# Pair 0 in transposed token order, a new order of all engines, and tiled matmuls grouped

## The chip, the cores and the metric

The kernel runs on one core of one Trainium2 chip. The metric is the device time of one execution in microseconds (us), as the median of several runs. Matmuls run on TensorE (PE; PEld is its loading of weights), copies, exps and gelus on ScalarE (ACT), element-wise work and 32x32 transposes on VectorE (DVE), some more on GpSimd (POOL). All transfers are issued by one queue, that of SyncE (SP).

## The reference

Batch `B = 8`, heads `H = 8`, tokens `S = 576`, head width 64. In each head 32 packed queries attend to all keys, and then the tokens attend to the 32 packed values. A gelu FFN over all 4608 tokens follows (`DM = 512`, `DFF = 2048`).

```python
p_packed = sm_attn(p, k, v)                 # per head: [32, 64]
out = sm_attn(q, p_packed, p_packed)        # per head: [576, 64]
x = out.transpose(0, 2, 1, 3).reshape(B * S, H * D)
h = x @ w_in
g = 0.5 * h * (1 + erf(h / sqrt(2)))
return g @ w_out
```

## The kernel before

**Units and steps.** Work is cut into 4 pairs of batches and 4 blocks of 512 columns of DFF, so 16 units `u` with 8 steps each: step `n` from 0 to 127, 32 of them a pair. The second softmax is never multiplied with the packed values: these are folded into `w_in` (`packed_w_in`, matmuls `wps` L960, split for precision into two parts `wp` by ACT L971 and DVE L976), and the hidden product `h` (L1026) multiplies the softmax weights `a2T` with `wp`. Per step, `h` goes through gelu on ACT (`graw` L1049), a cast (`g` L1056) and a subtraction on DVE (L1058), and four output tiles `o` of each batch (three matmuls each, L1079 to L1081) and one edge tile `o_edge` that both batches of a pair share are multiplied with `w_out`. DVE adds them up in `acc` (L1140), and the rows are stored (L1144).

**Attention of a pair.** `load` brings k and q (L383 for pair 0, L393 for the rest), `load_values` brings v (L440 and L442). PE computes the first scores (`s1`, in `products` L485), ACT their exps (`softmax`, L572), PE turns them (`e1T`, L593 and L596), multiplies them with v (`pp`, L631) and turns the result (L645); then come the second scores (`s2`, L485 again), the exps (L726), and the transposes on DVE (L744, L752) that make `a2`. Pair 0 reads k and q by rows and turns them on PE, so its tokens come out in another order than they have in memory; the exps L572 of pair 0 and the transposes `in_order` of L744 and L752 put them back in order. In the other pairs DVE turns 32x32 blocks. Until pair 0's `a2` is split into two parts, its first hidden products run unsplit in full fp32 (L1017, "plain").

**Tiled and whole matmuls.** The matmuls `s1`, `s2`, `pp` and `wps` use a part of PE's array each (the trace shows forms 64\*32 and 128\*32); all others use the whole array (128\*128).

**What sets the order.** Before anything is emitted, a planner written in Python (`class Order`) plays the kernel through: each piece is an `Op(engine, cost, step, fn, takes)`, `cost` being a guess in us. An engine that is free takes, of its ops whose inputs are there, the one with the lowest `step` for which the buffers (`Ring`s, with as many buffers as memory has room for) are free. Constants give the latency between engines, the rate of the transfers and the cost of a change of ACT's table. The tables `FIRST` (pair 0), `LATER` (pairs 1 to 3) and `LEAD` (weights) hold the `step` of each piece. The order that comes out is then fixed: on the chip each engine runs its own list and waits on semaphores.

**Idle matmuls.** While the planner has nothing for PE before time 150 and until the output has begun, `keep_warm` emits a matmul of zeros (L999) into the next free PSUM buffer. A tile first named by such a matmul keeps the name "idle". PSUM has the rings `psum_o` (four buffers, output tiles) and `wide` (two buffers, two banks each: `h`, scores, `e1T`, `pp`, `wps`).

Of the kernel before, what the change touches and what calls it, by code (L numbers as in the profile page):

```python
# [47 lines left out]
IDLE, IDLE_END = 0.11, 150.0  # L48

# [3 lines left out]
    "p": (-36.9, -24.7),  # L53
    "k": (19.1, -16.7, 9.7, 17.4),
    "v": (38.2, 48.4, 60.2, 73.6),
    "q": (19.5, 34.4, 60.7, 32.0),
    "scores1": (12.9, -36.2),
    "softmax1": (15.7, 19.0, 8.2, 16.7),
    "packed": (-24.6, -1.0, 7.5, 28.7),
    "scores2": (26.1, 14.1),  # L60
    "softmax2": (11.1, 33.2, 30.2, 70.4),
    "weights2": (29.1, 67.4, 29.6, 48.1),
    "groups1": ((0, 1, 2, 3),),
# [68 lines left out]
class Op:  # L132
# [3 lines left out]
    def __init__(self, engine, cost, step, fn, takes=(), table=None, busy=True, port=False):  # L136
        self.engine, self.cost, self.step, self.fn = engine, cost, step, fn
        self.takes, self.table, self.busy = takes, table, busy

        self.port = (engine == POOL and cost > 0) or port  # L140


class Order:
# [4 lines left out]
    def __init__(self):  # L148
# [5 lines left out]
        self.port = 0.0  # L154
# [60 lines left out]

    def issue(self, engine):
        ready = self.ready[engine]
        for i, (_, _, op, go_on, begin) in enumerate(ready):
            if not op.takes or all(r.has_room(name, n if r is op.takes[0][0] else 0) for n, (r, name) in enumerate(op.takes)):
                del ready[i]  # L220
                break
        else:
# [8 lines left out]
        if engine == DMA:  # L231
            n, size = op.cost
            end = self.now
            for _ in range(n):
                end = max(end, self.under_way[-DMA_DEPTH])
                self.link = max(self.link, end + DMA_ISSUE + DMA_START) + size / n / DMA_RATE
                end += DMA_ISSUE
                self.under_way.append(max(self.link, end + DMA_START) + DMA_END)
            done = self.under_way[-1]
        else:  # L240
# [7 lines left out]
            if engine == PE:  # L248
                end = begin + self.clock(begin, op.cost, op.busy)
# [21 lines left out]
def packed_attention_gelu_ffn(ctx: ExitStack, tc: tile.TileContext, q, k, v, p, w_in, w_out, out):  # L271
# [37 lines left out]
    vraws = ring("vraw", 1, [P, 20 * D])  # L309
# [4 lines left out]
    e1ts = ring("e1T", 1, [P, 5, P])  # L314
# [65 lines left out]
    def load(bt, name, src, c, step):  # L380
# [14 lines left out]
        cost, fn = ((1, 590e3), rows) if bt.b < 2 else ((4, 1475e3), blocks)  # L395
# [38 lines left out]

    def load_values(s, step):
        heads = slice(4 * s.hh, 4 * s.hh + 4)

# [6 lines left out]
        s.v = yield Op(DMA, (2, 660e3), step, fn, [(s.v_ring, f"v_{s.n}")])  # L444
# [82 lines left out]
    def scores1_of_chunk(s, step):  # L527
# [4 lines left out]
            PE, 0.68, step,  # L532
# [3 lines left out]
            [(wide, f"s1_{s.n}")], busy=False)  # L536
# [23 lines left out]
    def softmax1(ss, step):  # L560
# [6 lines left out]
        def exps():  # L567
            for s in ss:
                src, dst = s.e1, s.e1
                if s.b < 2:  # L570
                    src, dst = s.t1[:, :, :HALF].rearrange("p e (t x) -> p e t x", t=NT), rows_in_order(s.e1)
                nc.scalar.activation(dst, src, AF.Exp, bias=mx[:, 1, s.i:s.i + 1], scale=SCALE, accum_out=s.z)  # L572

        yield Op(ACT, (1.6 if ss[0].b < 2 else 0.76) * n, step, exps, table="exp")
# [11 lines left out]
    def packed(s, step):  # L586
# [4 lines left out]
        def most(t):  # L591
            for i in range(4):
                nc.tensor.transpose(bank(t)[:, i * P:(i + 1) * P], s.e1[:, i:512:4], ident)  # L593

        def least(t):
            nc.tensor.transpose(t[:64, :P], s.e1[:, 512:S], ident)  # L596

        def both(t):
            most(t)
            least(t[:, 1])  # L600

        def copy_most(t):
            nc.scalar.copy(e1T[:, 0:4].rearrange("p t n -> p (t n)"), bank(t))

        def copy_least(t):
            nc.scalar.copy(e1T[:64, 4], t[:64, :P])

        def copy_both(t):
            copy_most(t)
            copy_least(t[:, 1])  # L610
# [605 lines left out]
```

## Time and profile before

| | |
|---|---|
| median of three runs | 743.86 us (742.77 to 744.17) |
| span of the profiled execution | 741.7 us |
| median of the runs less that span | 2.16 us |
| PE busy | 730.1 us, 98% |
| DVE, ACT, POOL busy | 396.2, 351.8, 155.7 us |
| transfers | 106.77 MB, mean 144 GB/s |

The span goes from the first to the last instruction of one profiled execution; the runs are whole executions. "Busy" counts from an instruction's start to its end, and the ends of matmuls are modelled, so a PE that is busy all the time can still lose time between matmuls. What a group of matmuls costs is therefore read from the starts: from its own to that of the next matmul. A row of a timeline holds start, length, engine, line, operation, output and inputs, the form of the matmul (rows\*columns of the array), the tile, and behind "x" how many records are in it.

### The profile page before, as it was taken

Reading aid. Unit: us, or ns where it says so; the run is one execution under the profiler, and the core shown is the slowest. Engines: PE = TensorE matmul, PEld = TensorE weight load, DVE = VectorE, ACT = ScalarE, POOL = GpSimd, SP = SyncE. Lnnn points to the kernel's source line nnn. Section 1 sums busy time; section 2 is a strip of 40 time slices with the busy share of each in tenths; the row PEclk is TensorE's granted clock in tenths of the full one; section 3 lists DMA queues with packets and bytes.
Section 4 is the critical chain, followed back from the end, with each engine's and each line's share of the span. In section 5 each row is a group of like instructions: output and inputs, shape, how many; then the busy total and the mean of one; then the engine's idle time right before and its main releaser. Section 6 shows DMA issues by size and latency. Waiting matters only on the chain.

```text
span 741.7 us, 13289 instructions
## 1 busy us (share of the span) xinstructions
PE 730.1 (98%) x5348; PEld 589.0 (79%) x5348; DVE 396.2 (53%) x599; ACT 351.8 (47%) x597; POOL 155.7 (21%) x331
## 2 busy tenths in 40 slices
PE   9999999999999999999999999999999999999997
PEld 6777787787877788878888878777877888888886
DVE  5779877977579433533358632362337822333332
ACT  4777765766355543353245543353325544323321
POOL 2353465534411111101101101100111111111110
PEclk9999999999999999999999999999999999999999
DMA  9969897497418992252413997073050604030111
GB/s 311 351 216 176 215 199 278 145 233 266 148 50 236 163 189 95 36 199 65 165 64 81 258 153 192 1 202 97 4 193 32 243 0 159 14 108 36 56 59 71
DMA packets 156157, 106.77 MB, mean 144 GB/s; under 512 B 123840, under 2 KB 132032, under 8 KB 156096
## 3 DMA queue, kind: packets, MB, share of 16 engines
q1 hardware_dynamic: 156096, 105.93, 53.9%
q8 instruction: 42, 0.69, 0.4%
q14 instruction: 19, 0.16, 0.1%
HBM read 83.89 MB, written 22.02 MB: 143 GB/s over the span
## 4 chain that ended last, share of the span: by engine, by line
PE 90%; DMA 3%; SPq 3%; ACT 2%; issue 1%; DVE 1%; ACTq 0%
PE h L1026 25%; PE o L1079 16%; PE o L1081 15%; PE o L1080 14%; PE wps L960 4%; PE idle L999 2%; PE s L485 2%; SPq L393 2%; PE o_edge L1079 2%; PE o_edge L1081 2%; PE o_edge L1080 2%; PE pp L631 2%; DMA p<-in_p_dram 1%; PE e1Tm L593 1%; PE h L1017 1%
## 5 line engine op out<-in xcount | busy, mean ns | idle before, releaser
L1026 PEld LDWEIGHTS h<-a2T,wp 128*128 128x128 f32 x1488 | 208.9, 188 | 11.9 <-ACT a2T L755 1.7
L1026 PE MATMUL h<-a2T,wp 128*128 128x288 f32 x1488 | 217.5, 295 | 0.0
L1049 ACT ACTIVATE graw<-h 128x576 f32<-128x576 f32 x127 | 82.8, 652 | 279.4 <-PE h L1026 239.8
L1079 PE MATMUL o<-w,g 128*128 128x512 f32 x508 | 207.1, 408 | 0.3 <-DVE acc L1140 0.3
L1058 DVE TENSOR_TENSOR g<-graw,g 128x512 fp32r<-128x512 f32 x128 | 95.6, 747 | 207.9 <-ACT g L1056 198.1
L1081 PE MATMUL o<-w,g 128*128 128x512 f32 x508 | 199.3, 392 | 0.0
L1080 PE MATMUL o<-w,g 128*128 128x512 f32 x508 | 198.5, 391 | 0.0
L1069 POOL CAST t<-graw 128x64 fp32r<-128x64 f32 x128 | 38.5, 301 | 501.2 <-ACT graw L1049 496.0
L1079 PEld LDWEIGHTS o<-w,g 128*128 128x128 f32 x508 | 95.3, 188 | 47.3 <-issue 16.4
L1081 PEld LDWEIGHTS o<-w,g 128*128 128x128 f32 x508 | 95.4, 188 | 22.1
L1080 PEld LDWEIGHTS o<-w,g 128*128 128x128 f32 x508 | 95.6, 188 | 15.2
L1140 DVE TENSOR_TENSOR acc<-o,acc 128x512 f32<-128x512 f32 x96 | 63.7, 684 | 51.6 <-PE o L1081 51.4
L1056 ACT CAST g<-graw 128x512 fp32r<-128x512 f32 x128 | 79.5, 621 | 2.8
L976 DVE TENSOR_TENSOR wp<-wps,wp 128x1024 fp32r<-128x1024 f32 (+1 forms) x32 | 38.0, 1187 | 22.5 <-ACT wp L971 22.4
L1070 POOL TENSOR_TENSOR t<-graw,t 128x64 fp32r<-128x64 f32 x128 | 45.0, 351 | 10.3
L971 ACT CAST wp<-wps 128x1024 fp32r<-128x1024 f32 (+1 forms) x32 | 31.5, 983 | 20.4 <-PE wps L960 20.4
L960 PE MATMUL wps<-w,pp 64*32 64x512 f32 (+1 forms) x528 | 34.7, 582 | 0.0
L895 ACT ACTIVATE wt<-wraw 128x512 f32<-128x512 f32 x32 | 21.8, 680 | 24.2 <-DMA wraw<-in_moe_w_in_dram 14.7
L999 PE MATMUL idle<-still 128*128 128x256 bf16 x220 | 30.5, 285 | 1.1 <-DVE still L353 1.1
L999 PEld LDWEIGHTS <-still 128*128 128x128 bf16 x220 | 21.4, 102 | 7.6 <-issue 3.3
L930 POOL TENSOR_TENSOR wt<-wt 128x512 int32<-128x512 int32 x16 | 22.3, 1394 | 22.8 <-DVE wt L908 21.7
L922 POOL TENSOR_TENSOR w<-wt 128x512 int32<-128x512 int32 x16 | 21.8, 1363 | 23.8 <-DVE wt L908 15.4
(130 smaller groups left out, 659.0 us busy)
## 6 DMA issues: line engine op xcount, KB each, us to landing
w<-ws SPq DMA_DIRECT2D x72, 512.0 KB, 5.9
ws<-w SPq DMA_DIRECT2D x24, 512.0 KB, 5.0
out_dram<-acc SPq DMA_DIRECT2D x36, 256.0 KB, 2.1
wraw<-in_moe_w_in_dram SPq DMA_DIRECT2D x16, 512.0 KB, 5.4
v<-in_v_dram SPq DMA_DIRECT2D x16, 512.0 KB, 4.3
wraw<-in_moe_w_out_dram SPq DMA_DIRECT2D x16, 512.0 KB, 5.8
k<-in_k_dram SPq DMA_DIRECT2D x48, 144.0 KB, 4.7
q<-in_q_dram SPq DMA_DIRECT2D x48, 144.0 KB, 4.7
```

What stands on the lines that cost most here:

```text
L960: nc.tensor.matmul(t[r0:r0 + 32, hh, :m], lhsT=pp[b][rows, hh, r0:r0 + 32], rhs=wi[u, hh][rows, g, cols], start=True, stop=True)
L999: nc.tensor.matmul(bank(t)[:, :256], lhsT=still[:, :P], rhs=still, start=True, stop=True)
L1026: nc.tensor.matmul(t[:, half, :HALF], lhsT=w[:, wpart, ch, fc], rhs=a2T[b, ch][:, apart, half * HALF:(half + 1) * HALF], start=ch == 0 and ...
L1049: lambda raw: nc.scalar.activation(raw.rearrange("p (a n) -> p a n", a=2), t[:, :, :HALF], AF.Gelu),
L1056: g = yield Op(ACT, 0.52, lead, lambda g: nc.scalar.copy(g[:, 0], main), [(gts, f"g_{n}")])
L1058: DVE, 0.6, lead, lambda: nc.vector.tensor_tensor(g[:, 1], main, g[:, 0].bitcast(F32), ALU.subtract),
L1069: nc.gpsimd.tensor_copy(dst[:, 0], side)
L1070: nc.gpsimd.tensor_tensor(dst[:, 1], side, dst[:, 0].bitcast(F32), ALU.subtract)
L1079: nc.tensor.matmul(t, lhsT=g[0], rhs=w[:, 0], start=first, stop=False)
L1080: nc.tensor.matmul(t, lhsT=g[0], rhs=w[:, 1], start=False, stop=False)
L1081: nc.tensor.matmul(t, lhsT=g[1], rhs=w[:, 0], start=False, stop=last)
L1140: yield Op(DVE, 0.6, n, lambda: nc.vector.tensor_tensor(a, x, a, ALU.add))
```

## The change

Line numbers of the changed kernel: `products` L534, `e1T` L635, L636 and L646, `pp` L676, `wps` L1013, idle L1052, plain `h` L1070, `h` L1079, `o` L1132 to L1134, exps L614 and L772, gelu L1102.

**Pair 0 in transposed order.** The exps of pair 0 write to an order in which both sides have a short stride, the exps are turned in six pieces of 96 columns (before: four of 128 and one of 64), v comes in one transfer on 96 partitions, `pp` is 24 matmuls of 96 rows a chunk (before: 16 of 128 and 4 of 64), and `a2` is made by block transposes as in the other pairs. The output rows are put in order by the stores, the edge tile's in two transfers.

**The planner.** Each op says whether it is `tiled`. An engine now may pass over the first op for one that `suits` (same kind of matmul, same ACT table, a free port), if its step is no more than `patience` later. Costs, transfer sizes and issue times are new numbers. Loads and weights are `held` until the output has reached a step. Pair 1 has a table `SECOND` of its own; in `LATER` the first exps come in two groups of two chunks (before: one of four), in `SECOND` the second exps come one by one.

```diff
+PE_SWITCH = 0.09
-    "groups1": ((0, 1, 2, 3),),
+    "groups1": ((0, 1), (2, 3)),
     "groups2": ((0, 1), (2, 3)),
...
+SECOND = {
+    "p": (-32.99, 15.92),
...
+    "groups1": ((0, 1, 2, 3),),
+    "groups2": ((0,), (1,), (2,), (3,)),
+}
+AHEAD = 12
+PATIENCE = {PE: -1.9, ACT: -11.4, DVE: -2.9, POOL: 20.5, DMA: 31.6}
+STEADY = {PE: 21.5, ACT: 28.3, DVE: -11.8, POOL: 5.9, DMA: 20.3}
...
-    "groups2": ((0,), (1,), (2,), (3,)),
+    "groups2": ((0, 1), (2, 3)),
...
+    def suits(self, op):
+        if op.engine == PE:
+            return op.tiled or not self.tiled
+        if op.engine == ACT:
+            return op.table in (None, self.table)
+        return not op.port or self.port <= self.now
...
     def issue(self, engine):
+        for i, (step, _, op, *_) in enumerate(ready):
+            if found is not None and step > ready[found][0] + self.patience[engine]:
                 break
+            suits = self.suits(op)
+            if (found is None or suits) and self.can_take(op):
+                found = i
+                if suits:
+                    break
...
-    vraws = ring("vraw", 1, [P, 20 * D])
+    vraws = ring("vraw", 1, [P, 24 * D])
-    e1ts = ring("e1T", 1, [P, 5, P])
+    e1ts = ring("e1T", 1, [P, 6, P])
...
-                    src, dst = s.t1[:, :, :HALF].rearrange("p e (t x) -> p e t x", t=NT), rows_in_order(s.e1)
+                    src = s.t1[:, :, :HALF].rearrange("p e (c t x) -> p e t x c", c=3, t=3)
+                    dst = s.e1.rearrange("p (t e x c) -> p e t x c", t=3, e=2, c=3)
...
+        def third(i0):
+            def product(t):
+                for i in range(3):
+                    cols = slice(96 * (i0 + i), 96 * (i0 + i) + 96)
+                    nc.tensor.transpose(t[:96, i * P:(i + 1) * P], s.e1[:, cols], ident)
...
-                lambda t: nc.vector.transpose(in_order(t) if s.b < 2 else blocks(t), s.e2),
+                DVE, 0.77, step, lambda t: nc.vector.transpose(blocks(t), s.e2),
...
+    def held(task, step):
+        if step >= 1:
+            yield reached[min(int(step), NU * 8 - 1)]
+        yield from task
...
+            if n == STEPS + NC4:
+                order.patience = STEADY
...
+                for r, m in ((0, P),) if i != 4 else ((0, 64), (64, 64)):
+                    b, n0 = divmod((r0 + r) // PK, NB32)
+                    rows = out[b * S:(b + 1) * S].rearrange("(x n) d -> n x d", n=NB32)[n0:n0 + m // PK]
+                    nc.sync.dma_start(rows, a[r:r + m])
...
+        mine = SECOND if pr == 1 else LATER
```

How the order moves is seen at three places. In the rows, the name behind the operation is the output tile, those behind the arrow are the inputs, and "x" counts like instructions in a row.

PE, where pair 0's output begins. Before, word for word (`idle_794` is the tile of `h_0`):

```order
L631 MATMUL idle_809<-v_1_1_646,e1T_1_1_783 32x64 x20
L999 LDWEIGHTS still_72
L999 MATMUL idle_849<-still_72 128x256
...
L1017 MATMUL idle_794<-a2_0_593,wp_0_0_84 128x288 x4
L645 MATMUL idle_849<-ident_71,pn_1_1_854 128x128
...
L1017 MATMUL h_1_876<-a2_0_593,wp_0_0_84 128x288 x4
L485 MATMUL s2_1_1_889<-qT_1_1_760,pp_1_691 32x288 x8
```

The same place in the change (`idle_714` is the tile of `h_0`):

```order
L1070 MATMUL idle_714<-a2_0_712,wp_0_0_84 128x288 x4
L676 MATMUL idle_752<-v_1_1_701,e1T_1_1_733 32x64 x24
L534 MATMUL s2_1_0_0_799<-qT_1_0_592,pp_1_742 32x288 x4
L534 MATMUL s2_1_0_1_800<-qT_1_0_592,pp_1_742 32x288 x4
L1070 MATMUL h_1_809<-a2_0_712,wp_0_0_84 128x288 x4
L691 MATMUL ppTm_1_1_828<-ident_71,pn_1_1_815 128x128
```

The first hidden product moves ahead of the last `pp` of pair 0; 163 idle matmuls stand ahead of it (before: 215), and the whole program has 165 of them (before: 220).

PE, in pair 1's last unit, where the weights `wps_8` of pair 2 and the last chunk `pp_5_1` are made. Before, apart from each other:

```order
L960 MATMUL wps_8_0_0_4336<-w_8_0_3711,pp_4_3831 32x512 x2
L960 MATMUL wps_8_0_0_4336<-w_8_1_4166,pp_4_3831 32x512 x2
L1079 MATMUL o_60_2_4353<-w_7_2_3689,g_60_4273 128x512
...
L1026 MATMUL h_63_4405<-a2T_3_1_3018,wp_7_1_4058 128x288 x6
L631 MATMUL pp_5_1_4429<-v_5_1_3965,e1T_5_1_4377 32x64 x20
L1079 MATMUL o_60_0_4311<-w_7_4_4130,g_62_4418 128x512
```

In the change, the one behind the other:

```order
L1079 MATMUL h_60_4257<-a2T_3_1_2879,wp_7_1_3974 128x288 x6
L676 MATMUL pp_5_1_4272<-v_5_1_4073,e1T_5_1_4222 32x64 x20
L1013 MATMUL wps_8_0_0_4299<-w_8_0_3919,pp_4_3607 32x512 x2
L1013 MATMUL wps_8_0_0_4299<-w_8_1_4016,pp_4_3607 32x512 x2
L1013 MATMUL wps_8_0_0_4299<-w_8_0_3919,pp_4_3607 32x512 x2
L1013 MATMUL wps_8_0_0_4299<-w_8_1_4016,pp_4_3607 32x512 x2
L1132 MATMUL o_56_0_4123<-w_7_5_4112,g_59_4248 128x512
```

PE goes from whole to tiled matmuls at 54 places of the change's list (before: 76).

ACT, at the first exps of pair 2 (`e1_4_0` to `e1_5_1`; a row ACT_TABLE_LOAD is a change of table). Before:

```order
L1049 ACTIVATE graw_49_3664<-h_49_3642 128x576
L572 ACT_TABLE_LOAD
L572 ACTIVATE e1_4_0_3191,st_4_0_3190<-e1_4_0_3191,mx_2_2832 128x576
L572 ACTIVATE e1_4_1_3193,st_4_1_3192<-e1_4_1_3193,mx_2_2832 128x576
L572 ACTIVATE e1_5_0_3138,st_5_0_3136<-e1_5_0_3138,mx_2_2832 128x576
L572 ACTIVATE e1_5_1_3140,st_5_1_3139<-e1_5_1_3140,mx_2_2832 128x576
L1056 CAST g_49_3721<-graw_49_3664 128x512
L971 CAST wp_6_1_3568<-wps_6_1_0_3691 128x1024
L1049 ACT_TABLE_LOAD
L1049 ACTIVATE graw_50_3755<-h_50_3736 128x576
```

In the change:

```order
L614 ACT_TABLE_LOAD
L614 ACTIVATE e1_4_0_3103,st_4_0_3097<-e1_4_0_3103,mx_2_2805 128x576
L614 ACTIVATE e1_4_1_3105,st_4_1_3104<-e1_4_1_3105,mx_2_2805 128x576
L1102 ACT_TABLE_LOAD
L1102 ACTIVATE graw_44_3380<-h_44_3354 128x576
L1109 CAST g_44_3402<-graw_44_3380 128x512
```

The other two chunks' exps have a table load of their own elsewhere; the whole program has 30 table loads (before: 22), of which 15 return to gelu (before: 11).

PE, right behind `h_50`, before: the product's gelu is the last ACT row of before above, and `e1Tm_4_0` takes the PSUM banks of that product.

```order
L1026 MATMUL h_50_3736<-a2T_2_1_2769,wp_6_0_3413 128x288 x6
L1079 MATMUL o_48_0_3705<-w_6_3_3336,g_49_3721 128x512
L1080 MATMUL o_48_0_3705<-w_6_3_3336,g_49_3721 128x512
L1081 MATMUL o_48_0_3705<-w_6_3_3336,g_49_3721 128x512
L593 MATMUL e1Tm_4_0_3757<-ident_71,e1_4_0_3191 128x128 x4
```

In the change `e1Tm_4_0` stands elsewhere; two hidden products stand behind each other at the end of unit 1, where `h_16` takes the banks of `h_15`:

```order
L1079 MATMUL h_15_1647<-a2T_1_0_985,wp_1_1_1171 128x288 x6
L1079 MATMUL h_15_1647<-a2T_1_1_1025,wp_1_1_1171 128x288 x6
L1079 MATMUL h_16_1665<-a2T_0_0_1004,wp_2_0_1450 128x288 x6
L1079 MATMUL h_16_1665<-a2T_0_1_967,wp_2_0_1450 128x288 x6
L1013 MATMUL wps_2_1_0_1683<-w_2_0_1437,pp_1_742 32x512 x2
```

`e1Tm_4_0` moves away from the product it shares banks with, and `h_16` comes to stand right behind such a product.

More of the change, by code (lines that the diff above doesn't have):

```diff
@@ L132, with __init__ @@
 class Op:
-    def __init__(self, engine, cost, step, fn, takes=(), table=None, busy=True, port=False):
+    def __init__(self, engine, cost, step, fn, takes=(), table=None, busy=True, port=False, tiled=False):
         self.engine, self.cost, self.step, self.fn = engine, cost, step, fn
-        self.takes, self.table, self.busy = takes, table, busy
+        self.takes, self.table, self.busy, self.tiled = takes, table, busy, tiled
         self.port = (engine == POOL and cost > 0) or port
@@ L231, in issue @@
         if engine == DMA:
-            n, size = op.cost
+            n, size, issue = op.cost if len(op.cost) > 2 else (*op.cost, DMA_ISSUE)
             end = self.now
@@ L248, in issue @@
             if engine == PE:
-                end = begin + self.clock(begin, op.cost, op.busy)
+                switch = 0.0 if self.tiled == op.tiled else PE_SWITCH
+                self.tiled = op.tiled if op.cost else self.tiled
+                end = begin + self.clock(begin, op.cost + (switch if op.cost else 0), op.busy)
             done = end
@@ L393, in blocks @@
                     nc.sync.dma_start(t[32 * i:32 * i + 32], view[j])
[L395 removed]
+        cost, fn = ((1, 570e3), rows) if bt.b < 2 else ((4, 1560e3, 1.02), blocks)
         bt.raw[name, c] = yield Op(DMA, cost, step, fn, [(xraws, f"{name}_{bt.n}_{c}")])
@@ L442, in fn @@
             nc.sync.dma_start(tail, v[s.b, heads, 512:S].rearrange("g p d -> p g d"))
-        s.v = yield Op(DMA, (2, 660e3), step, fn, [(s.v_ring, f"v_{s.n}")])
+        cost, fn = ((1, 640e3), sixths) if s.b < 2 else ((2, 900e3, 0.6), fn)
+        s.v = yield Op(DMA, cost, step, fn, [(s.v_ring, f"v_{s.n}")])
         fire(s.v_loaded)
@@ L493, in part @@
             t = yield Op(
-                PE, 0.68, step,
+                PE, 0.55, step,
                 lambda t: products(
                     (t[:, 0], t[:, 1]), lhs, lambda head: xTs[head // 2][:, head % 2, cols], (0, 1)),
-                [(wide, f"s{which}_{bt.n}_{half}")], busy=False)
+                [(wide, f"s{which}_{bt.n}_{half}")], busy=False, tiled=True)
             def fn():
@@ L619, in packed @@
         else:
-            yield [piece("e1Tm", 0.55, most, 0.58, copy_most), piece("e1Tn", 0.15, least, 0.25, copy_least)]
+            yield [piece(name, 0.33, fn, 0.48, copy) for name, (fn, copy) in (("e1Tm", third(0)), ("e1Tn", third(3)))]
         sms.give(s.e1_home)
         yield s.v_loaded
-        main, tail = values_of(s.v)
+        if s.b < 2:
+            main = sixths_of(s.v)
+            pieces = [(e1T[:96, i], main[:, :, i]) for i in range(6)]
+        else:
+            main, tail = values_of(s.v)
+            pieces = [*((e1T[:, i], main[:, :, i]) for i in range(4)), (e1T[:64, 4], tail)]
         def product(t):
-            for i in range(5):
+            for i, (lhs, rhs) in enumerate(pieces):
                 for g, head in enumerate(PLACES[s.hh]):
                     cols = slice(32 * g, 32 * g + 32)
-                    lhs, rhs = (e1T[:, i, cols], main[:, head, i]) if i < 4 else (e1T[:64, 4, cols], tail[:, head])
-                    nc.tensor.matmul(bank(t)[cols, :D], lhsT=lhs, rhs=rhs, start=i == 0, stop=i == 4)
-        t = yield Op(PE, 0.85, step + 1, product, [(ring_, f"pp_{s.n}")], busy=False)
+                    nc.tensor.matmul(
+                        bank(t)[cols, :D], lhsT=lhs[:, cols], rhs=rhs[:, head], start=i == 0, stop=i == len(pieces) - 1)
+        t = yield Op(PE, 0.15 * len(pieces), step + 1, product, [(ring_, f"pp_{s.n}")], busy=False, tiled=True)
         e1ts.give(e1T)
@@ L669, in scores2_of_chunk @@
         ts = yield Op(
-            PE, 0.68, step,
+            PE, 0.55, step,
             lambda *ts: products(
                 banks(*ts), lambda n, g, head: pp[s.b][:, s.hh, 32 * g:32 * g + 32],
-                lambda head: xT[:, head], (s.hh, s.hh)), takes, busy=False)
+                lambda head: xT[:, head], (s.hh, s.hh)), takes, busy=False, tiled=True)
         ts = ts if len(takes) > 1 else [ts]
@@ L743, in weights2 @@
             yield Op(
-                DVE, 1.24, step, lambda: nc.vector.transpose(in_order(raw), s.e2))
+                DVE, 0.77, step, lambda: nc.vector.transpose(blocks(raw), s.e2))
             sms.give(s.e2_home)
@@ L962, in product @@
                             rhs=wi[u, hh][rows, g, cols], start=True, stop=True)
-        t = yield Op(PE, 0.16 + 0.87 * m / FB, step, product, [(wide, f"wps_{u}_{j}_{part}")], busy=False)
+        t = yield Op(PE, 0.07 + 0.87 * m / FB, step, product, [(wide, f"wps_{u}_{j}_{part}")], busy=False, tiled=True)
         for i in range(2):
@@ L1169, in packed_attention_gelu_ffn @@
             else:
-                start(weight(
-                    u, i, *([use + k - LEAD[name] for k in range(parts_of(i))] for name in ("load", "decode"))))
+                start(held(weight(
+                    u, i, *([use + k - LEAD[name] for k in range(parts_of(i))] for name in ("load", "decode"))),
+                    8 * u - AHEAD))
             if i < 2:
```

149 lines of the change are left out of this document (81 added, 68 removed).

## Prediction

> **What bounds the kernel.** I read the page's head and shares first, the chain next, then PE's waits, and at last the timelines where a wait or a change of tile form stands.
>
> ```profile
> span 741.7 us, 13289 instructions
> PE 730.1 (98%) x5348; PEld 589.0 (79%) x5348; DVE 396.2 (53%) x599; ACT 351.8 (47%) x597; POOL 155.7 (21%) x331
> PEclk9999999999999999999999999999999999999999
> PE 90%; DMA 3%; SPq 3%; ACT 2%; issue 1%; DVE 1%; ACTq 0%
> ```
>
> TensorE is busy for 98% of the span, at the full clock in each of 40 slices, and 90% of the chain is PE. So the time is the sum of what PE executes plus what it loses between matmuls. A faster VectorE or ScalarE is worth only what it takes off PE's list or off PE's waits. The sum below is made against this execution's span of 741.7 us; the median of the runs, 743.86 us, lies 2.16 us above it, and I add these 2.16 us again at the end. A change under 0.2% (1.5 us) is not told from none by runs like these.
>
> What PE waits for, from the view of waits (engine, line, releaser, us in total, times, longest):
>
> ```profile
> PE e1Tm L593 <- ACT graw L1049: 2.8, 2, 1.4
> PE s L485 <- ACT graw L1049: 1.6, 2, 0.8
> PE idle L999 <- DVE still L353: 1.1, 1, 1.1
> PE pp L631 <- DMA v<-in_v_dram: 0.8, 1, 0.8
> PE pp L631 <- ACT kT L424: 0.6, 1, 0.6
> PE idle L457 <- DMA p<-in_p_dram: 0.5, 1, 0.5
> PE o L1079 <- DVE acc L1140: 0.3, 1, 0.3
> ```
>
> All PE waits together are 7.7 us. What else the change can shorten is work that produces nothing, the idle matmuls, and the ways in and out of tiled blocks, which PE counts as busy.
>
> **Idle matmuls: 55 fewer.** The group of them, and one stretch of the chain:
>
> ```profile
> L999 PE MATMUL idle<-still 128*128 128x256 bf16 x220 | 30.5, 285 | 1.1 <-DVE still L353 1.1
> 23.50 1.97 PE idle L999 x18
> 25.00:50.00 25.00, 25.00 (x379) 18.98 (x376) 20.50 (x40) 18.28 (x41) 12.11 (x12) 1.00 0.83 283
> ```
>
> The 285 ns of the group overlap; 18 in a row take 1.97 us, so one costs 0.109 us. The change emits 165 and not 220: 55 x 0.109 = -6.0 us, if PE has not to wait in their place. The third row (busy time of PE, PEld, DVE, ACT and POOL, then clock, DMA share and GB/s) says what could make it wait between 25 and 50 us: VectorE at 20.50 of 25, ScalarE at 18.28, transfers at 0.83. All three are near full there, so PE's start hangs on their work; and the change shortens that work: four exps and four transposes of pair 0.
>
> ```profile
> L572 ACT ACTIVATE e<-s,mx 128x576 f32<-128x576 f32 x3 | 4.0, 1349 | 2.1 <-DVE mx L565 2.1
> L572 ACT ACTIVATE e<-e,mx 128x576 f32<-128x576 f32 x12 | 9.2, 766 | 1.0 <-DVE mx L565 1.0
> ```
>
> An exp with the long stride takes 1349 ns (three in this row, the fourth has a tile named idle), one in plain order 766: four times 0.58 is 2.3 us off ScalarE, and the transposes lose their long stride likewise. These lie on the way from the first scores to the first hidden product, ahead of which 163 idles now stand (215 before). I take the whole 6.0, with 0 as the other end; the rival below is that end.
>
> **Pair 0's extra matmuls.** Four more transposes and 16 more `pp` matmuls.
>
> ```profile
> 151.49 0.90 PE L631 MATMUL pp<-v,e1T 128*32 128x64 f32 x40
> 152.32 0.75 PE L593 MATMUL e1Tm<-ident,e 128*128 128x128 f32 x4
> 152.91 0.27 PE L596 MATMUL e1Tm<-ident,e 128*64 128x128 f32 x1
> ```
>
> From start to start four transposes take 0.59 us, so 0.15 each: +0.6. A chunk's `pp` takes 0.83 us for 40 records (20 matmuls of two records), 0.021 each: 32 more records are at most 0.7. No row shows a `pp` of 96 rows throughout, without the change from 128 to 64 rows inside; I take +0.3 between 0 and 0.7. The reordered stores of pair 0, one transfer more for the edge tile, cost PE nothing: SP issues them behind the pair's last `acc`, and what queues behind them on SP are loads that PE needs much later.
>
> **Tiled blocks grouped: 22 fewer entries (76 to 54).** A block alone, and two in one:
>
> ```profile
> 302.81 0.72 PE L485 MATMUL s<-kT,pT 64*32 64x288 f32 x16
> 303.46 0.50 PE L1079 MATMUL o<-w,g 128*128 128x512 f32 x1
> 303.79 0.39 PE L1080 MATMUL o<-w,g 128*128 128x512 f32 x1
> 203.42 0.39 PE L1080 MATMUL o<-w,g 128*128 128x512 f32 x1
> 203.64 0.39 PE L1081 MATMUL o<-w,g 128*128 128x512 f32 x1
> 203.96 1.20 PE L485 MATMUL s<-qT,pp 64*32 64x288 f32 x32
> 205.09 0.50 PE L1079 MATMUL o<-w,g 128*128 128x512 f32 x1
> 205.43 0.40 PE L1080 MATMUL o<-w,g 128*128 128x512 f32 x1
> ```
>
> Whole matmuls follow each other at 0.22 us (203.42 to 203.64). The last one before the tiled block takes 0.32 to the next start: 0.10 for the way in. The first one behind it takes 0.33 (303.46 to 303.79): 0.11 for the way out. The block of 16 itself takes 0.65, the one of 32 takes 1.13, so the second half adds 0.48 and not 0.65. A block that joins another saves between 0.21 (both ways) and 0.38 (0.17 inside as well). Of the 22, by the order, 2 lie among the idle matmuls and are worth nothing, 10 join a block of the same form (64\*32, mostly `wps` to scores), and 10 join a `pp` (128\*32). I take 10 x 0.30 = 3.0 for the same form. For the other form no row of before shows two neighbours: its bounds are 0 (each change of form costs the same) and 0.38; I take the 0.21 of the ways in and out, rounded to 2.0 for ten. Together -5.0, with ends of -2.1 and -7.6. [...]
>
> **Waits for gelu on a shared bank.** The two largest entries of the waits, 2.8 and 1.6 us, are four places of one kind:
>
> ```profile
> 254.37 1.75 PE L1026 MATMUL h<-a2T,wp 128*128 128x288 f32 x12
> 256.20 0.65 ACT L1049 ACTIVATE graw<-h 128x576 f32<-128x576 f32 x1 [3.34 <-issue]
> 256.90 0.72 PE L485 MATMUL s<-kT,pT 64*32 64x288 f32 x16 [0.79 <-ACT graw L1049]
> 321.65 1.28 ACT L1049 ACT_TABLE_LOAD   x1 [1.77 <-PE h L1026]
> 322.94 0.65 ACT L1049 ACTIVATE graw<-h 128x576 f32<-128x576 f32 x1
> 323.64 0.74 PE L593 MATMUL e1Tm<-ident,e 128*128 128x128 f32 x4 [1.38 <-ACT graw L1049]
> ```
>
> The scores go to the PSUM banks of the hidden product just finished and wait for its gelu, 0.79 us. In the other kind three `o` matmuls lie between, but ScalarE must load the gelu table (1.28) first, and that load starts only when the product is there: 1.38 us. Twice each makes 4.4. In the change's order I looked for the same pattern. Two places have nothing between (`h_15` to `h_16`, and `h_28` to scores of pair 1): 2 x 0.8. Two have three `o` between and no table load: 3 x 0.23 = 0.7 of the 0.8 is covered, so 0.1 each. Behind every gelu table load stand at least twelve `o` (12 x 0.23 = 2.8 us against 1.28 + 0.65 + 0.2 = 2.1). So 1.8 us of waits are left: -2.6, with ends of -4.4 and 0 (as many new places as old).
>
> **The rest.** I keep the waits for v, kT, p and `acc` (2.2 us). v has one buffer, and its load takes 5.40 us:
>
> ```profile
> 159.69 5.40 DMA v<-in_v_dram
> ```
>
> In the order its tightest use in the change lies a little farther from the one ahead than in before, but p comes later in the queue: so no change, with 0 and twice 2.2 as ends. Eight more table loads are work of ScalarE, busy for 47%, and cost nothing as long as the `o` matmuls behind each cover it (rival 3 if not). Loads held until a step of the output cost nothing if they still come before their use: the transfers' share is 0.55 in a stretch of steady work,
>
> ```profile
> 200.00:250.00 50.00, 50.00 (x381) 40.20 (x380) 37.86 (x60) 26.59 (x40) 6.15 (x20) 1.00 0.55 143
> ```
>
> so a load that is issued later finds room there; what would be late is seen as a wait for DMA.
>
> The tail (the last twelve edge matmuls, `acc`, store) stands as it was.
>
> Sum: -6.0 + 0.6 + 0.3 - 5.0 - 2.6 = -12.7, so a span of 729.0, and 731.2 us with the 2.16.
>
> **Rivals.**
> (1) The idles' time comes back. The start is bound by transfers, VectorE and ScalarE, not by the count of idles that a planner emits; if its costs are too low, PE waits where the idles were. For it: the 0.83 of the transfers between 25 and 50 us, and the `kT` wait of 0.6. Against: the shorter exps. Time: 731.2 + 6.0 = 737.2.
> (2a) A change between the forms 128\*32 and 64\*32 costs what a change to the whole array costs. Then the ten joins with `pp` save nothing, and the time is 731.2 + 2.0 = 733.2. For it: PE's `pp` rows stand between whole matmuls everywhere here, so nothing speaks against it. [...]
> (2b) Grouping saves nothing at all: 736.2. Against it: the 1.13 of the double block.
> (3) Slower: table loads. There are 30 and not 22.
>
> ```profile
> L1049 ACT ACT_TABLE_LOAD x11 | 14.1, 1283 | 6.1 <-PE h L1026 5.1 <-PE h L1017 0.9
> 314.01 1.28 ACT L572 ACT_TABLE_LOAD   x1
> 313.34 0.66 ACT L1049 ACTIVATE graw<-h 128x576 f32<-128x576 f32 x1 [3.03 <-PE h L1026]
> ```
>
> Each of the 15 returns to gelu could stall PE as at 323.64, by 1.38 us, if the product's gelu is needed at once: 731.2 + 15 x 1.4 = 752. From ten such stalls on it is slower than before (731.2 + 9 x 1.4 = 743.8). Against it: the twelve `o` behind each, and a ScalarE that is busy for 47%. Nothing lies between the gelu that ends at 314.00 and the load at 314.01. [...]
> (4) All waits vanish and joins save their most: 731.2 - 2.6 - 1.8 - 2.2 = 724.6.
>
> **Chances.** Forecast 0.50 (its own range 728 to 734); rival 2a 0.20 and 2b 0.07; rival 1 0.14, as three resources are near full at the start; rival 3 0.06, of which 0.02 ends within 0.2%; rival 4 0.03. The range takes in 1, 2a and 2b, with 1.3 above them for two at once in part, and goes most of the way to 4: 725.5 to 738.5. It leaves out rivals 3 and 4, and some 0.05 of cases where 1 and 2 come together. Faster 0.94, same 0.02, slower 0.04.
>
> **What the profile after would show.** The group of idles with 165 matmuls, PE's wait list up to 60 us not longer than before (else rival 1); 54 entries into tiled blocks, joined blocks adding 0.17 us less each than alone, and PE's busy time some 10 us lower; waits for gelu of about 1.8 us in two to four places; 30 table loads, none followed by a PE wait of 1.4 (else rival 3). The prediction is wrong if the clock's row shows less than 9 at the start, where fewer idles stand, or if a transfer that is held until late comes too late for its first use: a PE wait for DMA in the middle of the span.

## The result: 1% slower, and the profile after

The changed kernel takes 751.86 us (748.51 to 752.99) against 744.17 us of the kernel before: a ratio of 1.0099, with a 95% interval of 1.0077 to 1.0122. The forecast was 731.2 us, so it missed by 20.7 us and had the wrong sign. One later run, of the kernel with four stores below, took 1182.62 us at a granted clock of 0.557 where its other five took 735 to 738, and is left out here; the recorded expectation that calls this kernel 736.1 us still counts it.

The head of the page after, its clock row and its chain:

```profile
span 746.7 us, 13261 instructions
...
PE 722.5 (97%) x5329; PEld 588.6 (79%) x5329; DVE 401.8 (54%) x606; ACT 359.0 (48%) x603; POOL 149.0 (20%) x328
...
PEclk9999999999999899999999999999999999999999
...
PE 86%; DMA 7%; SPq 3%; DVE 2%; issue 1%; ACT 0%; ACTq 0%; DVEq 0%
```

PE is busy for 7.6 us less than before (722.5 against 730.1; the forecast wanted some 10), and still the span is 5.0 us longer. One slice of the clock has an 8, and the transfers' share of the chain has gone from 3% to 7%. So the work became shorter and the waits longer. PE's waits after:

```profile
PE pTm L506 <- DMA p<-in_p_dram: 4.8, 1, 4.8
PE o L1132 <- DMA w<-ws: 3.7, 1, 3.7
PE pp L676 <- DMA v<-in_v_dram: 3.0, 1, 3.0
PE idle L506 <- DMA p<-in_p_dram: 2.2, 2, 1.4
...
PE s L534 <- ACT graw L1102: 0.8, 1, 0.8
PE h L1079 <- ACT graw L1102: 0.7, 1, 0.7
```

Three waits for transfers, 11.5 us together, stand out; the kernel before has one of this kind, 0.8 us for v. In the timeline of PE they begin at 207, 235 and 252 us, and behind two of them the `o` matmuls start 0.42 us apart (241.00 to 241.42) where 0.23 is usual:

```profile
209.80 0.90 PE L676 MATMUL pp<-v,e1T 128*32 128x64 f32 x40 [2.95 <-DMA v<-in_v_dram]
...
240.11 0.66 PE L506 MATMUL pTm<-ident,p 128*128 128x128 f32 x2 [4.76 <-DMA p<-in_p_dram]
...
241.00 0.63 PE L1133 MATMUL o<-w,g 128*128 128x512 f32 x1
241.42 0.63 PE L1134 MATMUL o<-w,g 128*128 128x512 f32 x1
...
256.24 0.65 PE L1132 MATMUL o<-w,g 128*128 128x512 f32 x1 [3.71 <-DMA w<-ws]
```

The windows say why (busy PE, PEld, DVE, ACT, POOL; then clock, transfers' share, GB/s):

```profile
211.00:214.00 3.00, 3.00 (x18) 2.59 (x17) 0.95 (x2) 2.97 (x6) 0.00 (x0) 1.00 0.26 102
208.25:209.75 1.50, 0.00 (x0) 0.00 (x0) 1.15 (x2) 0.36 (x1) 0.56 (x2) 1.00 0.27 101
241.00:246.00 5.00, 5.00 (x16) 4.23 (x15) 3.54 (x5) 0.00 (x0) 0.00 (x0) 0.50 0.41 88
256.60:259.60 3.00, 3.00 (x8) 2.30 (x7) 0.00 (x0) 0.00 (x0) 0.00 (x0) 0.50 0.40 86
```

From 241 to 246 and from 256.6 to 259.6 us the granted clock is 0.50: the `o` matmuls there start 0.42 us apart and not 0.23. And in the second row PE does nothing, waits for v_3_1, and the share of the 16 DMA engines is only 0.27, as much as about four of them make (0.27 x 16 = 4.3, an estimate). All three waits lie between 200 and 257 us, where the queue holds pair 0's stores:

```profile
200.87 0.69 SPq L1208 DMA_DIRECT2D out_dram<-acc  x1
...
204.78 3.48 SPq L1208 DMA_DIRECT2D out_dram<-acc  x3
...
227.44 1.23 SPq L1208 DMA_DIRECT2D out_dram<-acc  x2
228.72 0.83 SPq L488 DMA_DIRECT2D v<-in_v_dram  x1
...
230.58 2.75 SPq L500 DMA_DIRECT2D p<-in_p_dram  x2
...
240.36 3.08 SPq L1208 DMA_DIRECT2D out_dram<-acc  x4
```

### The profile page after: what moved, and what is told of

The parts are those of the page before. It is cut to its first block, busy times and chain, and to the rows that moved or that the text cites. A ratio compares the mean times of both kernels' runs of the same rounds, so it can differ in the third digit from the quotient of the medians.

```text
span 746.7 us, 13261 instructions
## 1 busy us (share of the span) xinstructions
PE 722.5 (97%) x5329; PEld 588.6 (79%) x5329; DVE 401.8 (54%) x606; ACT 359.0 (48%) x603; POOL 149.0 (20%) x328
## 4 chain that ended last, share of the span: by engine, by line
PE 86%; DMA 7%; SPq 3%; DVE 2%; issue 1%; ACT 0%; ACTq 0%; DVEq 0%
PE h L1079 24%; PE o L1132 16%; PE o L1134 15%; PE o L1133 14%; PE wps L1013 4%; DMA v<-in_v_dram 2%; DMA p<-in_p_dram 2%; PE s L534 2%; PE o_edge L1132 2%; PE o_edge L1134 2%; PE o_edge L1133 2%; DMA w<-ws 2%; SPq L433 2%; PE pp L676 1%; PE idle L1052 1%; PE e1Tm L635 1%
## 5 line engine op out<-in xcount | busy, mean ns | idle before, releaser
L1102 ACT ACTIVATE graw<-h 128x576 f32<-128x576 f32 x127 | 82.7, 651 | 296.1 <-PE h L1079 224.7
L1079 PEld LDWEIGHTS h<-a2T,wp 128*128 128x128 f32 x1488 | 210.1, 189 | 12.0 <-ACT graw L1102 2.6
L1079 PE MATMUL h<-a2T,wp 128*128 128x288 f32 x1488 | 218.1, 296 | 0.7 <-ACT graw L1102 0.7
L1132 PE MATMUL o<-w,g 128*128 128x512 f32 x512 | 208.5, 407 | 3.7 <-DMA w<-ws 3.7
L1134 PE MATMUL o<-w,g 128*128 128x512 f32 x512 | 201.9, 394 | 0.7 <-DVE g L1111 0.7
L1133 PE MATMUL o<-w,g 128*128 128x512 f32 x512 | 201.8, 394 | 0.0
L1122 POOL CAST t<-graw 128x64 fp32r<-128x64 f32 x128 | 35.3, 276 | 501.4 <-ACT graw L1102 364.4
L1132 PEld LDWEIGHTS o<-w,g 128*128 128x128 f32 x512 | 96.9, 189 | 41.8 <-issue 20.8
L1134 PEld LDWEIGHTS o<-w,g 128*128 128x128 f32 x512 | 97.0, 189 | 23.3 <-DVE g L1111 1.1
L1133 PEld LDWEIGHTS o<-w,g 128*128 128x128 f32 x512 | 97.0, 189 | 15.4
L1013 PE MATMUL wps<-w,pp 64*32 64x512 f32 (+1 forms) x528 | 34.2, 580 | 0.2
L449 DVE STREAM_TRANSPOSE kT<-k 128x1152 f32<-128x1152 f32 x12 | 16.4, 1371 | 20.0 <-DMA k<-in_k_dram 20.0
L961 DVE SCALAR_TENSOR_TENSOR wt<-wraw,wt 128x512 int32<-128x512 int32 x32 | 25.0, 781 | 0.6
L1132 PE MATMUL o_edge<-w,t 128*128 128x512 f32 x64 | 25.2, 394 | 0.0
```

The costliest lines, as they stand in the source:

```text
L1013: nc.tensor.matmul(t[r0:r0 + 32, hh, :m], lhsT=pp[b][rows, hh, r0:r0 + 32], rhs=wi[u, hh][rows, g, cols], start=True, stop=True)
L1079: nc.tensor.matmul(t[:, half, :HALF], lhsT=w[:, wpart, ch, fc], rhs=a2T[b, ch][:, apart, half * HALF:(half + 1) * HALF], start=ch == 0 and ...
L1102: lambda raw: nc.scalar.activation(raw.rearrange("p (a n) -> p a n", a=2), t[:, :, :HALF], AF.Gelu),
L1122: nc.gpsimd.tensor_copy(dst[:, 0], side)
L1132: nc.tensor.matmul(t, lhsT=g[0], rhs=w[:, 0], start=first, stop=False)
L1133: nc.tensor.matmul(t, lhsT=g[0], rhs=w[:, 1], start=False, stop=False)
```

## The experiments

Where the order of the engines had to stay as it is, a kernel was built whose planner first notes the order of all pieces and then emits them in that order, with the moves shown. Ratios are to the kernel before, measured on the same chip. The kernels with outer dimensions of 8 and 16, with more idles and with loads first ran on another chip than the other eight: there before took 742.72 us, and 743.63 and 743.38 with the others. A difference between kernels of the two chips is therefore uncertain by about 1 us.

**Late loads, stores, or neither.** My first theory (A) was that SP's list has the loads in a bad order; its rivals were the reordered stores (B) and the order of the engines' own work (C).

p_4 ahead of v_4_0:

```diff
+    place(notes, "p_4", ahead_of="v_4_0")
```

> The changed kernel with its lists kept piece by piece, except that on SP's list the load p_4 stands ahead of v_4_0 and not behind it. Theory A (late transfers: PE stalls 4.8 us at 235 us for p_4, which waits behind 576 KB of v_4_0, and the TensorE clock is then halved for 6.8 us): the wait at pTm for p falls from 4.8 us to under 1 and the halved stretch behind it goes, 4.8 + 3.0 = 7 to 8 us less at that place; some of it comes back as a longer wait for the weights at 250 us (3.7 now, 3 to 8 then). In all 741 to 749 us against 751.9. Theory B (pair 0's reordered stores hold the queue): the wait stays over 3 us, since the two stores ahead are still ahead; 750 to 753. Theory C (the loss lies in the order of the engines' own work): no change, 751 to 753.

Measured 751.58 us, 1.0104 (1.0088 to 1.0120). Theory A missed: the wait for p fell only to 2.5, and the one for the weights rose. B had expected more than 3 for p and missed that too; the time fits B and C alike.

```profile
PE o L1132 <- DMA w<-ws: 8.2, 1, 8.2
...
PE pTm L506 <- DMA p<-in_p_dram: 2.5, 1, 2.5
```

The same, and four weights ahead of k_5_1 and of the stores:

```diff
+    place(notes, "p_4", ahead_of="v_4_0")
+    for name in ("w_4_4", "w_4_5", "w_5_2", "w_5_3"):
+        place(notes, name, ahead_of=((168, 33), 1201, 0))   # the first of the last three stores
+    place(notes, "k_5_1", behind="w_5_3")
```

> As the one before (p_4 ahead of v_4_0), and the four weight loads w_4_4, w_4_5, w_5_2, w_5_3 ahead of the load k_5_1 and of the last three stores of pair 0. Theory A: both waits for transfers between 235 and 257 us (4.8 and 3.7) fall under 1 us and no slice of the span has less than full clock: 13 us less than the changed kernel, 736 to 741 us. Some risk that kT on VectorE now waits for k_5_1 and holds back what is behind it there, 1 to 4 us. Theory B: 746 us or more, as the waits only move behind the stores. Theory C: 751 to 753.

Measured 748.68 us, 1.0062 (1.0046 to 1.0078). The wait for the weights is gone, but those for v (3.0) and p (2.5) stay, k_5_1 now comes late on VectorE, and 4.6 us of waiting for `a2T` stand in its place; the 736 to 741 of theory A didn't come, and B's 746 or more did.

```profile
PE h L1079 <- DVE a2T L802: 4.6, 1, 4.6
```

Pair 0's rows stored as one block:

```diff
-                if pr > 0:
+                if pr >= 0:
                     nc.sync.dma_start(out[r0:r0 + P], a)
                     return
```

> The changed kernel, with pair 0's rows stored in the order in which they lie in the accumulators (as the other pairs' are), so that the output's rows of pair 0 come out in another order than the reference's; same bytes, one transfer fewer. Theory A: the waits for v_3_1, p_4 and the weights stay within 1 us of 3.0, 4.8 and 3.7; 748 to 753 us. Theory B: the waits shrink by half or more and the time falls to 740 to 746.

Measured 731.50 us (731.29 to 732.28), 0.9837 (0.9824 to 0.9850), below even theory B's 740. PE's waits for v_3_1, p_4 and the weights aren't in its list at all, which begins so (the first two rows are the page's head):

```profile
span 729.5 us, 13260 instructions
PE 717.8 (98%) x5329; PEld 585.2 (80%) x5329; DVE 403.1 (55%) x606; ACT 359.0 (49%) x603; POOL 148.3 (20%) x328
...
PE idle L506 <- DMA p<-in_p_dram: 1.7, 2, 0.9
PE h L1070 <- DVE wp L1029: 1.5, 1, 1.5
...
PE idle L676 <- ACT e1T L649: 0.9, 1, 0.9
```

So the form of pair 0's stores costs 751.86 - 731.50 = 20.4 us (19.8 when each is taken against before as measured with it), and without it the change gains 12.1. The two profiles show 17.2 of this (spans 746.7 and 729.5): 11.5 are the three waits, and 4.7 are PE's longer busy time (722.5 against 717.8), with the clock at 0.50 in two stretches. The profiled run of the change was its fastest, 748.51 us; what the other 3 us of its median are, no profile shows.

Idle matmuls in the wait for p_4:

```diff
+    i = next(i for i, (_, k) in enumerate(notes) if k == "pTm_4")
+    notes[i:i] = [(PE, "idle wide")] * 42
```

> The changed kernel with 42 idle matmuls (0.109 us each, 4.6 us) ahead of pTm_4, where PE otherwise waits 4.8 us for p_4. They fill the wait and nothing is moved. If the halved clock behind the wait is caused by PE standing still, the stretch of 6.8 us at half clock from 239 us goes and the time falls by about 3 us, to 746 to 750 us, with the wait itself at most 1 us. If the clock was lowered by something else (or only by chance), it stays and the time is the same, 750 to 753.

Measured 751.19 us, 1.0103 (1.0087 to 1.0118). At the filled wait the clock stays at 1.00 (first row), which fits a clock lowered by PE's standing still; but PE then comes earlier to the weights, waits 7.3 us there, and the halved clock follows that wait (second row). The 3 us weren't won.

```profile
238.00:246.00 8.00, 7.90 (x62) 6.61 (x61) 3.09 (x7) 1.27 (x2) 0.56 (x2) 1.00 0.65 123
258.50:265.00 6.50, 3.73 (x9) 2.96 (x10) 0.00 (x0) 0.00 (x0) 0.00 (x0) 0.50 0.32 72
```

**What about the stores is slow.** They differ from whole ones in two things: the rows lie apart in memory, and the outer dimension of the transfer is 4 (2 at the edge tile), not 128. Four kernels tell these apart.

Four transfers of 32 rows each, the same rows to the same places:

```diff
-                    nc.sync.dma_start(rows, a[r:r + m])
+                    for k in range(m // PK):
+                        nc.sync.dma_start(rows[k], a[r + PK * k:r + PK * k + PK])
```

> The changed kernel, with each reordered store of pair 0 (4 x 32 rows, 4 the outer dimension) issued as four transfers of 32 rows: the same rows to the same places, every list else as it was. Theory B1 (a store whose outer dimension is 4 is carried by 4 of the 16 DMA engines, and later loads wait behind it on these four): up to 16 packets in flight in the stores, the waits for v_3_1, p_4 and the weights under 0.5 us each, 731 to 734 us. Theory B2 (rows that lie 36 KB apart in memory are slow to write): the waits stay, 745 to 753 us.

Measured 735.44 us (735.10 to 737.83), 0.9890 (0.9870 to 0.9911). B2 is out: the rows lie as far apart as in the change. B1 fits, but the time is 1.4 us above its range: SP now issues four times as many transfers, and waits of 1.5 (p_4) and 1.2 (weights) are left.

```profile
203.19 1.76 SPq L1209 DMA_DIRECT2D out_dram<-acc  x4
...
236.86 6.09 SPq L1209 DMA_DIRECT2D out_dram<-acc  x12
```

The kernel before with the changed kernel's stores in pair 0:

```diff
-            yield Op(DMA, (1, 262e3), n, lambda: nc.sync.dma_start(out[r0:r0 + P], a))
+            yield Op(DMA, (1, 262e3), n, store)    # store() as in the change
```

> The kernel before, with pair 0's stores (and only these) given the changed kernel's form, so that the rows of pair 0 come out in another order than the reference's. By B1 the loads behind the stores come 3 to 5 us later as in the change: a wait for p_4, which has 5.4 us between its issue and its use in before, of 2 to 5 us, one for the weights behind it, and some 3 us of halved clock: 748 to 756 us. If the change's late loads come from its own order of SP's list (theory A, already weak), before stays under 745.5.

Measured 756.97 us, 1.0177 (1.0155 to 1.0200): 13.6 us more than before, by this one edit and with an order of SP's list that never had late loads. Before, p_4 and p_5 weren't waited for at all here.

```profile
PE pTm L457 <- DMA p<-in_p_dram: 9.3, 2, 5.5
```

Outer dimensions of 8 and 16:

```diff
-                for r, m in ((0, P),) if i != 4 else ((0, 64), (64, 64)):
...
+                nc.sync.dma_start(out[r0:r0 + P].rearrange("(x n) d -> n x d", n=8), a)     # and n=16
```

> The changed kernel with pair 0's stores as one transfer each whose outer dimension is 8 (8 x 16 rows; the rows of a tile are permuted within the tile's own 256 KB, so they come out in another order than the reference's). Theory B1 (the outer dimension sets how many DMA engines carry a store): at most 8 packets of 2 KB in flight in the first store, which takes half the time it takes with 4; the three waits for transfers fall to a third or less: 733 to 742 us, between the 731.5 of whole stores and the 751.9 of the change. If engines have nothing to do with it and any store that isn't one whole block is slow: 748 to 753.

> As the one before, with 16 as the outer dimension (16 x 8 rows). B1: 16 packets in flight, no wait for a transfer over 0.5 us between 200 and 260 us, 730.5 to 733 us, the same as whole stores. Otherwise 748 to 753.

Measured 739.58 us, 0.9954 (0.9940 to 0.9968), with 8, and 732.05 us, 0.9850 (0.9836 to 0.9863), with 16. Stretches with little but stores under way, from the kernels with 8, with 16 and with whole stores (the row of the change with 4 is above, 211 to 214 us):

```profile
209.00:211.50 2.50, 2.50 (x16) 2.09 (x15) 0.98 (x2) 2.47 (x5) 0.17 (x1) 1.00 0.53 205
```

```profile
207.00:208.50 1.50, 1.50 (x44) 1.21 (x44) 1.43 (x3) 1.49 (x2) 0.00 (x0) 1.00 1.02 380
```

```profile
206.50:207.75 1.25, 1.25 (x43) 0.98 (x35) 1.18 (x3) 1.24 (x2) 0.00 (x0) 1.00 1.10 413
```

The share of the 16 engines is 0.26, 0.53, 1.02 and 1.10, and the rate 102, 205, 380 and 413 GB/s. 16 times the share is 4.2, 8.5, 16.3 and 17.6, as if 4, 8, 16 and 16 engines worked (an estimate; no view here counts the engines of a transfer). With 8 the waits for v (1.0) and the weights (none) fell as expected, that for p only from 4.8 to 2.6. What is shown is that share, rate and time go with the outer dimension: 751.86 us with 4, 739.58 with 8, 732.05 with 16 and 731.50 with whole stores.

**The forecast's other terms.** 23 joined pairs of tiled blocks separated, over the kernel of the four stores:

```diff
+    for a, b in zip(pe, pe[1:]):
+        if a in tiled and b in tiled:      # all but the five joins of the start
+            place(notes, whole, ahead_of=b)   # the next whole group of PE's list
```

> The changed kernel with the four transfers a store, and 23 of its joined pairs of tiled blocks (all behind the start) separated: the next whole matmuls are pulled ahead of the second block; the other lists stay. By the forecast's price (5.0 us for 20) this adds 5.8 us: 737 to 739 against 731 to 734 without. By the rival that only joins of one form save (2a), it adds 3.5: 735. By rival 2b nothing: the same as with the joins.

Measured 742.73 us, 0.9992 (0.9980 to 1.0004), against 735.44 with the joins: 7.3 us for 23, or 0.32 each. The forecast's price was 0.25. Nine of the 23 join a `pp`; if those saved nothing, as rival 2a has it, the other 14 would have to save 0.52 each, more than the 0.38 that the prediction worked out as their most. So 2a, whose price here was 3.5 us, and 2b are out. In this join of the change, the step from 128\*32 to 64\*32 costs next to nothing: 36 records of `pp` in the first form take 0.64 us, 0.018 each (0.017 in pair 0's uniform `pp`, 48 in 0.81, shown further down), and the scores start right then, at 347.98, ahead of the last four of `pp`, which have their form.

```profile
347.34 0.84 PE L676 MATMUL pp<-v,e1T 128*32 128x64 f32 x36
347.98 0.45 PE L534 MATMUL s<-kT,pT 64*32 64x288 f32 x4
348.00 0.24 PE L676 MATMUL pp<-v,e1T 64*32 64x64 f32 x4
348.65 0.50 PE L1132 MATMUL o<-w,g 128*128 128x512 f32 x1
```

55 more idle matmuls, over the kernel with whole stores:

```diff
+    for i in reversed(spots[2::3]):      # spots: the places of the idle matmuls
+        notes.insert(i, notes[i])
```

> The changed kernel with whole stores for pair 0 (rows in another order than the reference's; 731.5 us), and behind every third idle matmul one more, 55 in all, so that there are 220 as in before. If PE bounds the start, as the forecast's term of the idles says, 55 x 0.109 = 6.0 us are added: 736.5 to 738.5. If other engines and transfers bound it (the forecast's rival 1), PE's waits of the start (some 5 us) shrink instead, and 731.5 to 733.5 come out.

Measured 734.51 us, 0.9886 (0.9872 to 0.9899): 3.0 us more than without them (3.9 when each is taken against before on its own chip), between the two expectations. The first hidden product starts 2.63 us later, not 6.0 (first row with whole stores alone, second with the idles as well), and the waits of the start for p and `e1T`, 2.6 us in the list of the whole stores, are gone from its list.

```profile
44.36 2.11 PE L1070 MATMUL idle<-a,wp 128*128 128x288 f32 x8
```

```profile
46.99 2.11 PE L1070 MATMUL idle<-a,wp 128*128 128x288 f32 x8
```

Small moves over the four stores:

```diff
+    place(notes, ((168,), 1152, 86), ahead_of="s2_2_0")   # an output group
+    place(notes, ((168,), 1152, 46), ahead_of="h_16")     # an output group
+    place(notes, "p_1", ahead_of="wraw_0_2_0")
+    place(notes, "p_0", ahead_of="wraw_0_0_1")
```

> The changed kernel with the four transfers a store, and four small moves: one output group pulled ahead of h_16 and one ahead of s2_2_0, which both wait 0.7 to 0.8 us for a gelu on their bank, and the loads p_0 and p_1 one and two places earlier on SP's list. If PE bounds everything, the two bank waits (1.5) go, and 0 to 1.7 of the waits for p: 728.5 to 731.5. If the start is bound by VectorE, the earlier p only makes the wait for wp longer, and 1.2 to 1.5 us are all: about 730.

Measured 736.88 us, 0.9908 (0.9890 to 0.9925): 1.4 us more than 735.44, and the expectation missed. The two waits for gelu are gone, but a new one of 0.7 stands among the matmuls of the start, q comes late where p came late, and others follow:

```profile
PE idle L460 <- DMA q<-in_q_dram: 3.0, 1, 3.0
...
PE pp L676 <- DMA v<-in_v_dram: 0.8, 1, 0.8
PE idle L676 <- ACT graw L1102: 0.7, 1, 0.7
```

**A version that beats both.** Four transfers a store, and on SP's list the urgent loads ahead of the stores:

```diff
+    place(notes, "p_4", ahead_of=((168, 31), 1201, 0))
+    for name in ("w_4_4", "w_4_5", "w_5_2", "w_5_3"):
+        place(notes, name, ahead_of=((168, 33), 1201, 0))
+    place(notes, ((168, 27), 1201, 0), behind="v_3_1")
```

> The kernel with four transfers a store (736.1 us; the right rows in the right places), and on SP's list the load p_4 ahead of the two stores that stand before it, the four weights ahead of the last three stores of pair 0, and v_3_1 ahead of the first store. The 1.76 us that SP needs to issue a store of four then holds back no load: the waits for p_4 (1.5), the weights (1.2) and v_3_1 (0.3) fall under 0.5 each: 731.5 to 734.5 us. If the rest of the difference to whole stores (4.6 us) comes from the writes themselves or from chance at the start, 735 to 737.

Measured 732.98 us (732.54 to 733.37), 0.9865 (0.9849 to 0.9880), with the change's rows in the change's places: 1.4% faster than before. No wait for v_3_1, p_4 or the weights is in its list. Of the 3.9 us between four stores and whole ones (735.44 and 731.50), 2.5 are won (1.8 when each kernel is taken against before on its own chip), so about half of that difference, or a little more, came from loads that stood behind SP's issuing of stores.

## Why the prediction was wrong, point by point

- **The step that failed** is "The reordered stores of pair 0, one transfer more for the edge tile, cost PE nothing". It counted transfers and their place in SP's queue, and not the rate at which a store of this form runs. It was mis-sized by 20.4 us (0 against 751.86 - 731.50). Its second half, "what queues behind them on SP are loads that PE needs much later", was wrong as well: p_4 was needed 4.8 us after its issue (issued at 230.58, PE ready at 235.35). The prediction shows no row for such a transfer and gives this term no bounds, as it does for its other terms that no row shows. What the runs showed in its place: a store with 4 as its outer dimension moves 102 GB/s at 0.26 of the engines, against 413 at 1.10 for a whole one, the loads behind it come late, and PE waits 11.5 us for them and works at half clock in two stretches behind the waits.
- **Idle matmuls**, -6.0 forecast: 55 of them are worth 3.0 to 3.9 (734.51 against 731.50, on two chips). Rival 1 was about half true: transfers (p, 1.7) and ScalarE (`e1T`, 0.9) take a part of it back as waits at the start; VectorE does not, its 1.5 for `wp` is there with and without the 55. The prediction called all three near full at the start, but ScalarE's 18.28 of 25 us is 0.73.
- **Joins**, -5.0 forecast: 0.32 each, so -6.3 for 20.
- **Waits for gelu**, 4.4 to 1.8 forecast: 4.4 to 1.5 measured, at the two zero-gap places that were named (0.8 and 0.7).
- **Pair 0's extra matmuls**, +0.9 forecast, are nearly free in the timeline of the change. Six transposes of 96 columns take 0.65 us from start to start (38.30 to 38.95), and the five of before 0.59 (46.22 to 46.70, 47.25 to 47.36); a `pp` of 48 records takes 0.81 (40.24 to 41.05), and one of 40 took 0.83. Over the four chunks that is about +0.1. No run measures it by itself.

```profile
38.30 0.49 PE L646 MATMUL idle<-ident,e 128*96 128x128 f32 x3
...
38.95 1.36 PE L1052 MATMUL idle<-still 128*128 128x256 bf16 x11
40.24 0.88 PE L676 MATMUL idle<-v,e1T 96*32 96x64 f32 x48
41.05 1.20 PE L460 MATMUL qm<-ident,q 128*128 128x128 f32 x9
```

- **Table loads** (rival 3) stall nothing: no wait of 1.4 us for gelu is in the list after, with 30 loads.
- **The sum without the stores** came out at 731.50 against 731.2, and that is partly luck, because errors cancel: the idles were worth 2 to 3 us less, the joins 1.3 more, the extra matmuls cost 0.8 less and the gelu waits shrank by 0.3 more. With these sizes the sum is -3.0 - 6.3 - 2.9 + 0.1 = -12.1 (-13.0 with 3.9 for the idles), against -12.1 measured with whole stores (731.50 to the 743.63 of before on that chip).
- **The signs to look for** were half right: a wait for DMA in mid-span came, but not from loads that are held until late (the kernel before with the changed stores has it too), and the clock row's 8 stands in mid-span behind such a wait, not at the start where the prediction looked for it.

## What to carry to other kernels

When a transfer's access pattern changes, read its outermost dimension as well as its bytes and its place in the queue: stores with 4 and 8 there ran at a share of 0.26 and 0.53 of the DMA engines (102 and 205 GB/s, against 413 for whole ones), and loads behind them came late, even though nobody was waiting for the stores themselves. Splitting the store in four brought 751.86 us to 735.44 here but cost the issuing queue time (1.76 us for four against 0.69 for the one), so put loads that PE needs soon ahead of it (732.98). Where PE is the bound, a late load costs its wait and can cost more: behind waits of 3.7 and 4.8 us in the change the clock was at 0.50 for 3.4 and 6.8 us.

## What was unexpected of the hardware

Stores of 256 KB in rows of 2 KB ran at 102, 205 and 380 GB/s with outer dimensions of 4, 8 and 16. The halved clock depends on more than the length of the wait: in the change, 2.95 us of standing still at 207 us left it at 1.00 (first row), and a wait of 3.0 us for the same load in the kernel with p_4 first was followed by 0.50 (second row).

```profile
209.80:213.00 3.20, 3.20 (x51) 2.56 (x52) 0.69 (x1) 2.20 (x4) 0.00 (x0) 1.00 0.28 107
```

```profile
211.60:214.60 3.00, 3.00 (x44) 2.37 (x44) 0.68 (x1) 1.57 (x3) 0.00 (x0) 0.50 0.28 108
```

What else it goes with can be read from the granted clock in narrow windows. In the change it falls at 239.37, rises at 246.20, falls at 256.44 and rises at 259.85 us: 6.83, 10.24 and 3.41 apart, all multiples of 3.41. In the kernel with p_4 first, the clock is 1.00 in the two stretches of 3.41 us that end at 211.44 and 242.16 (the last two rows below), and behind both the `o` matmuls start 0.43 us apart (213.89 to 214.32, 242.47 to 242.90): the two ends are 30.72 apart, nine times 3.41, with a start of their own. Cut into stretches along this grid, from 200 to 260 us, the change's two at full clock with PE busy for 0.00 and 0.20 us (third and fourth row of the next block) are followed by 0.50, and each of its others at full clock, busy for 1.61 or more, by full clock. The wait of 2.95 us is shared by two stretches (the first two rows, busy 1.61 and 2.26), and the one of 3.0 falls nearly whole into one (the next to last row, 0.45). A wait of 2.5 us for p in the same kernel lay mostly in one stretch (last row, 1.23), and the clock fell behind it.

```profile
205.24:208.65 3.41, 1.61 (x10) 1.13 (x9) 3.18 (x6) 3.33 (x4) 0.00 (x0) 1.00 0.66 209
208.65:212.06 3.41, 2.26 (x46) 1.86 (x47) 1.16 (x2) 1.27 (x3) 0.56 (x2) 1.00 0.28 105
235.96:239.37 3.41, 0.00 (x0) 0.00 (x0) 0.00 (x0) 0.09 (x1) 0.14 (x1) 1.00 0.42 92
253.02:256.44 3.42, 0.20 (x1) 0.20 (x2) 0.69 (x1) 0.87 (x2) 0.56 (x2) 1.00 0.64 127
```

```profile
208.03:211.44 3.41, 0.45 (x2) 0.01 (x1) 2.79 (x5) 2.19 (x3) 0.56 (x2) 1.00 0.43 158
238.75:242.16 3.41, 1.23 (x7) 1.09 (x8) 0.79 (x2) 0.40 (x1) 0.37 (x2) 1.00 0.56 116
```
